# Softmax weights of forty steps transposed in 32x32 blocks by VectorE and regrouped through DRAM, in a fused attention and Fourier-mixing kernel

## The chip, the cores and the metric

The kernel runs on one core of a Trainium2 chip. The metric is the device time of one execution in microseconds (us). The median of three runs is 1605.03 us (1603.99 to 1605.74). One further execution was profiled; it took 1605.7 us, and its span, from the first to the last instruction of the profile, is 1603.8 us. All times of single instructions come from that execution.

## The reference

The inputs are q, k and v of shape (8 batches, 8 heads, 576 positions, 64), a scalar tau, w_ch1 (512 x 2048) and w_ch2 (2048 x 512), all in float32. In short:

```python
scores = matmul(q, k.transpose(0, 1, 3, 2)) / 8
scores = where(scores >= max(scores, -1) - tau, scores, -1e9)
attn = exp(scores - max(scores, -1))
x = matmul(attn / (sum(attn, -1) + 1e-9), v)      # heads side by side: (8, 576, 512)
u = x + real(fft(fft(x, axis=1), axis=2))
un = (u - mean(u, -1)) / sqrt(var(u, -1) + 1e-6)
out = u + maximum(un @ w_ch1, 0) @ w_ch2
```

## The kernel before

**Attention.** Two heads make a pair, and four pairs a batch, so there are 32 pairs. A pair is worked off in five steps (NT = 5): steps t = 0 to 3 hold 128 query positions of both heads, step 4 the last 64 positions of both heads side by side. A step n,t has the number i = 5n + t. For each step, `scores` multiplies q by k into PSUM (L427, L433 for step 4). `softmax_first` takes the row maxima on VectorE (L506) and the exponentials on ScalarE (L512, and L516 for the threshold). `softmax_second` applies the threshold and sums on VectorE (L527, L531, L534). `softmax_third` divides by the sum on ScalarE (L540). `weights_in_parts` then transposes the weights on TensorE, one block of 128x128 at a time: the tile `pe` (L578) holds the last 64 keys of both heads, and two tiles `pw` (L596) the 512 others of each head. That makes nine transposes a step, five for step 4. ScalarE copies them to SBUF (L584, L598, L600). `values_in_parts` multiplies them by v (L627): the first part, for positions 0 to 255, needs steps 0 and 1, the second part steps 2, 3 and 4.

**Mixing.** When the four pairs of a batch are done, their rows are folded by symmetry (`fold_rows`, L660), and `mixing` (L719) does both Fourier transforms with tables on TensorE and writes u, transposed, into the ring `u_t`.

**The two products with w1 and w2.** The 4608 rows of u are worked off in nine groups of 512. Group 0 uses plain products (`channels`). Groups 1 to 8 use `two_level`, a Strassen-Winograd scheme. For w1 it is one level: the product is split in four parts, and each part in seven blocks, m = 1 to 7, in the order of the list `ORDER`. Each block multiplies one combination of quarters of w1 by one combination of the tokens (b, t1, t2, t3, minus_t4), as four matmul calls at L1163, which the profile shows as eight instructions. `u_form` makes the combinations of tokens, on GpSimd except in the last two groups. Blocks 1, 6 and 7 share one bank of PSUM. Block 1 is copied out by ScalarE (L1172), as are blocks 5 (L1174) and 4 (L1182). Blocks 2, 6, 7 and 3 are added to the result by VectorE (L1100), and ScalarE applies the maximum with zero (L1105). The product with w2 has two levels, 49 blocks of four calls (L1306), with m in the order `L1` outside and `J` inside. There m = 1, 5 and 4 are copied by ScalarE (L1321), m = 2 is added by VectorE (L1323), and the others also by VectorE (L1326).

**Loads of the weights.** The combinations of w1 and w2 are made once (`w1_forms`, `w2_forms`), kept in DRAM as f1 and f2, and loaded again in each group into a ring of three buffers w1[0] to w1[2], of four blocks each (`PER = 4`, L1026; the loads are issued by `ensure`, L1030, at L1036). `block` asks for load n+2 when load n is first used.

**What sets the order of the work.** The order is written out by hand: every engine runs its instructions in the order of the program, and so does SP, from whose queue nearly all DMAs are issued. The pools decide only which buffer a tile gets. PSUM has four banks of tag `mm` for everything but scores, and four of tag `sc` for scores. From batch 3 on (counting from 1), the loop at L1635 runs one step of attention in each iteration and mixes in the other work: `fill` advances the products by a budget of work (`per_slot`) three times an iteration. Within an iteration i the order is: scores of i; the first or second part of the values, at t = 3 for the pair itself and at t = 1 for the pair before; maxima and exponentials; a first `fill`; weights and sums; the first half of the transposes of step i-1; a second `fill`; the second half; the division for step i; at t = 3 the transposes of q and k by VectorE (`prep_pair`, L398 to L401); a third `fill`. At t = 2 the transfers of v of the next pair are issued (`load_v`), and at t = 4 those of q and k of the pair after the next (`load_pair`), eight transfers together. After the second part of the values, `swap_rows` (L645) exchanges two rows of odd pairs by two DMAs out and two back, issued together.

After the last step of attention, at about 1370 us, the products of groups 7 and 8 run alone.

Of the kernel before, what the change touches and what calls it, by code (L numbers as in the profile page):

```python
# [47 lines left out]
def kernel(  # L48
# [48 lines left out]
    v_in = [const.tile([128, 10, D], FP32, name=f"v_in{u}") for u in range(2)]  # L97

# [24 lines left out]
    def load_pair(n, queue=nc.sync):  # L123
# [4 lines left out]
        raws = []  # L128
        for src, name, eng in ((q, "q_in", nc.sync), (k, "k_in", queue)):
# [10 lines left out]
            raws.append(raw)  # L140
        loaded[n] = raws
# [115 lines left out]
    w1 = [const.tile([128, HID], FP32, name=f"w1_{c}") for c in range(ND)]  # L257
# [181 lines left out]
    def softmax(i, between=None, meanwhile=None, behind=None):  # L439
# [43 lines left out]
        if normalized(i // NT):  # L483
            nc.vector.tensor_scalar(
                out=e[:, 0:S], in0=e[:, 0:S], scalar1=den[:, 0:1], scalar2=None, op0=ALU.mult
            )
            if nh == 2:
                nc.scalar.activation(
                    out=e[:, S : 2 * S], in_=e[:, S : 2 * S], func=ACT.Copy, scale=den[:, 1:2]
                )  # L490
        else:
            rec = sb.tile([128, 2 * D], FP32, tag="rec", name="rec")
            nc.gpsimd.tensor_copy(
                rec[:, :].rearrange("p (j d) -> p j d", j=nh), _repeated(den[:, 0:nh], 2 * D // nh)
            )
# [51 lines left out]

    def transposed_weights(i):
# [3 lines left out]
    def weights_in_parts(i):  # L552

        n, t = divmod(i, NT)
        e, rec = steps.pop(i)
        if t in (0, 2):
# [3 lines left out]
            e_t = sb.tile([128, 8, S - 256], FP32, tag="e_t", bufs=1, name="e_t")  # L560
            ends = sb.tile([128, 2, S - 256], FP32, tag="ends", bufs=1, name="ends")
            vt = heads[n][2]
            if t == 0 and PAIRS[n % NPAIR] % 2:

                vt = sb.tile([128, 10, D], FP32, tag="vr", bufs=1, name="v_rev")
                src = heads[n][2]
                nc.gpsimd.tensor_copy(vt[:, :, 0:1], src[:, :, 0:1])
                last = src[:, :, D - 1 : D]
                down = bass.AP(
                    tensor=last.tensor, offset=last.offset,  # L570
                    ap=[list(last.ap[0]), list(last.ap[1]), [-1, D - 1]],
                )
                nc.gpsimd.tensor_copy(vt[:, :, 1:D], down)
# [6 lines left out]
        if rec is not None:  # L580
            nc.tensor.transpose(pe[:, 1, :], rec[:, :], ident[:, :])
# [23 lines left out]
    def values_in_parts(n, part):  # L605
# [19 lines left out]
        for c in range(5):  # L625
            for j in range(2):
                nc.tensor.matmul(  # L627
                    pv[64 * j : 64 * j + 64, 0:m], vt[:, 2 * c + j, :],
                    e_t[:, 4 * j + c, 0:m] if c < 4 else ends[:, 0, 0:m],
# [3 lines left out]
        if normalized(n):  # L633
# [8 lines left out]
        if not (late and n % NPAIR == 0):  # L642
            swap_rows(n)

    def swap_rows(n):  # L645
        b, p = n // NPAIR, PAIRS[n % NPAIR]
        x = xs[b][p]
        if p % 2:
# [4 lines left out]
            for j in range(2):  # L653
                nc.sync.dma_start(out=x[64 * j : 64 * j + 1, :], in_=swap[1 - j : 2 - j, :])
# [217 lines left out]
    def channels(rows):  # L872
# [18 lines left out]
        def both():  # L891
            yield from w1_forms()
            ensure(1)
# [27 lines left out]
    ORDER = (1, 2, 5, 6, 4, 7, 3)  # L921
# [6 lines left out]
    def w1_forms():  # L928
# [6 lines left out]
        def keep(m, at):  # L935
            to = f1[:, :, :].rearrange("p (part m) (c n) -> p m c part n", m=7, c=2)
            for c in range(2):
                nc.sync.dma_start(
                    out=to[:, ORDER.index(m), c],
                    in_=quarters[at][c].rearrange("p (part n) -> p part n", n=256),  # L940
                )
# [23 lines left out]
        ensure(0)  # L965
# [60 lines left out]
    PER = 4  # L1026
    LOADS = [(f1, 28, k) for k in range(0, 28, PER)] + [(f2, 49, k) for k in range(0, 49, PER)]
    issued = 0

    def ensure(n):  # L1030

        nonlocal issued
        while issued <= n and issued < (NG - 1) * len(LOADS):
# [3 lines left out]
                out=w1[issued % 3][:, 0 : 512 * n_blocks].rearrange("p (j n) -> p j n", n=512),  # L1037
# [4 lines left out]
    def block(g, second, index):  # L1042

        n = len(LOADS) * (g - 1) + (7 if second else 0) + index // PER
        if index % PER == 0:
            ensure(n + 2 if g > 1 or second or index < 20 else n + 1)
        return w1[n % 3][:, 512 * (index % PER) : 512 * (index % PER + 1)]

# [13 lines left out]
    def two_level(g, rows):  # L1062
# [22 lines left out]
        def u_form(out_, in0, in1):  # L1085
            for c in range(2):
                (nc.vector if g >= NG - 2 else nc.gpsimd).tensor_tensor(
# [60 lines left out]
        for part in range(4):  # L1148
# [3 lines left out]
            sum_ = None  # L1152
            for at, m in enumerate(ORDER):
                left = block(g, False, 7 * part + at)
                if m in (6, 7):
                    bank = sum_
                else:
                    bank = ps.tile([128, 512], FP32, tag="mm", bufs=4, name="ph")
                if m == 1:
                    sum_ = bank  # L1160
                for q in range(2):
                    for c in range(2):
                        nc.tensor.matmul(  # L1163
                            bank[:, 256 * q : 256 * q + 256].rearrange(
                                "p (two n) -> p two n", two=2
                            ),
                            left[:, 256 * c + 128 * q : 256 * c + 128 * q + 128], right[m][:, c],
                            start=q == 0 and c == 0 and m not in (6, 7), stop=c == 1,
                            skip_group_check=True,
                        )  # L1170
                if m == 1:
# [572 lines left out]
```

## Time and profile before

| What | us |
|---|---|
| median of three runs | 1605.03 |
| the profiled execution: its time | 1605.7 |
| its span | 1603.8 |
| VectorE busy | 1105.6 |
| ScalarE busy | 908.4 |
| GpSimd busy | 811.7 |
| transposes of the weights (L596 and L578), as listed | 172.1 + 45.2 |
| row maxima (L506) and threshold (L527) from batch 3 on | 154.0 + 168.1 |
| DMA engines: mean share of the largest queue | 49.1% |

The page lists for each engine its busy time, then groups of instructions with their count, their sum, the mean of one in ns, the idle time of the engine just ahead of them, and what ended most of that idle time. A busy TensorE is not TensorE at its peak, since its instructions overlap: one starts before the one ahead of it has ended. Hence starts are compared with starts where the question is what an instruction takes from the engine. A window gives the busy time of each engine within a stretch of the span. The granted clock of TensorE was 0.988 over the span.

### The profile page before, as it was taken

Reading aid. Unit: us, or ns where it says so; the run is one execution under the profiler, and the core shown is the slowest. Engines: PE = TensorE matmul, PEld = TensorE weight load, DVE = VectorE, ACT = ScalarE, POOL = GpSimd, SP = SyncE. Lnnn points to the kernel's source line nnn. Section 1 sums busy time; section 2 is a strip of 40 time slices with the busy share of each in tenths; the row PEclk is TensorE's granted clock in tenths of the full one; section 3 lists DMA queues with packets and bytes.
Section 4 is the critical chain, followed back from the end, with each engine's and each line's share of the span. In section 5 each row is a group of like instructions: output and inputs, shape, how many; then the busy total and the mean of one; then the engine's idle time right before and its main releaser. Section 6 shows DMA issues by size and latency. Waiting matters only on the chain.

```text
span 1603.8 us, 27061 instructions
## 1 busy us (share of the span) xinstructions
PE 1537.4 (96%) x9770; PEld 1189.2 (74%) x9770; DVE 1105.6 (69%) x2165; ACT 908.4 (57%) x1873; POOL 811.7 (51%) x1014
## 2 busy tenths in 40 slices
PE   8999979999999999999999999999999999999997
PEld 4555445555787778877787878787887778879997
DVE  7997886845869566766577566856676656746547
ACT  5774665554655666656666666656665665223121
POOL 6784664034455552536254724455263625537646
PEclk9999999999999999999999999999999999999998
DMA  6423221555956264634564355626463534546655
GB/s 158 131 57 115 75 76 36 175 158 164 291 159 203 72 182 125 182 104 141 141 175 140 113 159 145 191 69 180 123 185 108 154 113 158 191 157 237 235 193 190
DMA packets 245499, 239.05 MB, mean 149 GB/s; under 512 B 196947, under 2 KB 214869, under 8 KB 225014
## 3 DMA queue, kind: packets, MB, share of 16 engines
q1 hardware_dynamic: 242854, 237.02, 49.1%
q8 instruction: 78, 1.28, 0.3%
q10 hardware_dynamic: 2512, 0.30, 0.2%
q14 instruction: 55, 0.45, 0.1%
HBM read 207.50 MB, written 29.62 MB: 148 GB/s over the span
## 4 chain that ended last, share of the span: by engine, by line
PE 76%; DVE 14%; ACT 4%; issue 2%; POOL 2%; DMA 1%; SPq 0%; DVEq 0%; ACTq 0%; POOLq 0%
PE ph L1163 24%; PE po L1306 17%; PE pv L627 8%; PE sc L427 7%; PE pw L596 6%; PE po L901 4%; PE ph L877 2%; PE py L750 2%; DVE e L467 2%; PE sc L433 1%; PE pa L767 1%; PE pe L578 1%; PE pa L771 1%; DVE neg L451 1%; ACT e L512 1%
## 5 line engine op out<-in xcount | busy, mean ns | idle before, releaser
L512 ACT ACTIVATE e<-sc,neg 128x576 f32<-128x576 f32 x216 | 158.6, 734 | 139.8 <-DVE neg L506 139.4
L506 DVE TENSOR_REDUCE neg<-sc 128x1 f32<-128x576 f32 x216 | 154.0, 749 | 112.0 <-PE sc L427 104.1
L1306 PE MATMUL po<-w,w_all 128*128 128x128 f32 x1792 | 229.1, 278 | 0.7 <-ACT ends L584 0.7
L1306 PEld LDWEIGHTS po<-w,w_all 128*128 128x128 f32 x1792 | 214.7, 193 | 10.2 <-issue 5.5
L1100 DVE TENSOR_TENSOR hs<-ph,hs 128x512 f32<-128x512 f32 (+1 forms) x128 | 105.1, 821 | 158.5 <-PE ph L1163 104.0
L1109 POOL TENSOR_TENSOR w<-hs 128x512 f32<-128x512 f32 x32 | 42.1, 1320 | 318.9 <-ACT hs L1105 245.1
L596 PE MATMUL pw<-ident,e 128*128 128x128 f32 x1152 | 172.1, 276 | 18.0 <-ACT x_first L634 9.1
L1163 PE MATMUL ph<-u_t,w 128*128 128x256 f32 x768 | 180.5, 381 | 0.5 <-DMA w<-f 0.4
L527 DVE SCALAR_TENSOR_TENSOR e<-sc,thr,e 128x576 f32<-128x576 f32 x216 | 168.1, 811 | 17.7 <-ACT thr L516 17.7
L427 PE MATMUL sc<-kT,qT 64*128 64x288 f32 x1024 | 170.3, 432 | 7.9 <-DVE e L467 7.9
L598 ACT COPY e_t<-pw 128x512 f32<-128x512 f32 x256 | 148.5, 594 | 45.8 <-PE pw L596 44.6
L540 ACT ACTIVATE e<-e,den 128x576 f32<-128x576 f32 x216 | 157.6, 775 | 16.6 <-DVE den L534 15.4
L596 PEld LDWEIGHTS pw<-ident,e 128*128 128x128 f32 x1152 | 136.3, 142 | 36.3 <-ACT x_first L634 10.1
L1163 PE MATMUL ph<-w_all,w 128*128 128x256 f32 x672 | 157.0, 382 | 2.9 <-DVE hs L1100 1.8
L1163 PEld LDWEIGHTS ph<-u_t,w 128*128 128x128 f32 x768 | 141.2, 190 | 23.4 <-issue 4.4
L1105 ACT ACTIVATE hs<-hs 128x512 f32<-128x512 f32 (+1 forms) x96 | 74.1, 772 | 122.0 <-DVE hs L1100 120.8
L1163 PEld LDWEIGHTS ph<-w_all,w 128*128 128x128 f32 x672 | 123.5, 190 | 25.6 <-issue 6.2
L427 PEld LDWEIGHTS sc<-kT,qT 64*128 64x128 f32 x1024 | 93.9, 186 | 62.9 <-issue 32.8
L1213 POOL TENSOR_TENSOR w_all<-w_all 128x128 f32<-128x128 f32 (+2 forms) x160 | 118.5, 758 | 29.9 <-DVE w_all L1326 22.4
L1306 PE MATMUL po<-w,hs 128*128 128x128 f32 x960 | 126.3, 279 | 0.0
L1306 PEld LDWEIGHTS po<-w,hs 128*128 128x128 f32 x960 | 116.2, 193 | 9.4 <-issue 7.2
L792 POOL TENSOR_TENSOR u_t<-x,tmp 128x289 f32<-128x289 f32 (+1 forms) x45 | 34.5, 766 | 104.8 <-DVE tmp L787 104.8
(221 smaller groups left out, 2985.1 us busy)
## 6 DMA issues: line engine op xcount, KB each, us to landing
w<-f SPq DMA_DIRECT2D x152, 1024.0 KB, 4.9
hs<-in_moe_w_ch_dram SPq DMA_DIRECT2D x23, 512.0 KB, 4.6
q_in<-in_q_dram SPq DMA_DIRECT2D x128, 72.0 KB, 3.9
out_dram<-u SPq DMA_DIRECT2D x36, 256.0 KB, 2.5
k_in<-in_k_dram SPq DMA_DIRECT2D x124, 72.0 KB, 3.0
v_in<-in_v_dram SPq DMA_DIRECT2D x64, 128.0 KB, 4.7
f<-w SPq DMA_DIRECT2D x14, 512.0 KB, 4.0
f<-w SPq DMA_DIRECT2D x7, 1024.0 KB, 4.4
```

Of the source, the lines that this page charges most:

```text
L427: nc.tensor.matmul(sc[j][:, c, 0:HALF], qT[hp, 128 * t : 128 * t + 128], kT[hp, k0 + HALF * c : k0 + HALF * (c + 1)], start=True, stop=True,)
L506: nc.vector.tensor_reduce(out=neg[:, j : j + 1], in_=sc[j][:, :, 0:HALF], axis=AXIS_XY, op=ALU.max, negate=True,)
L512: nc.scalar.activation(out=ej, in_=sc[j][:, :, 0:HALF], func=ACT.Exp, bias=neg[:, j : j + 1], scale=1.0)
L527: nc.vector.scalar_tensor_tensor(out=ej, in0=sc[j][:, :, 0:HALF], scalar=thr[:, j : j + 1], in1=ej, op0=ALU.is_ge, op1=ALU.mult, accum_out ...
L540: nc.scalar.activation(out=e[:, S * j : S * (j + 1)], in_=e[:, S * j : S * (j + 1)], func=ACT.Copy, scale=den[:, j : j + 1],)
L596: nc.tensor.transpose(pw[:, c, :], e[:, c0 : c0 + 128], ident[:, :])
L598: nc.scalar.copy(e_t[:, 4 * j : 4 * j + 4, qs], pw[:, :, :])
L627: nc.tensor.matmul(pv[64 * j : 64 * j + 64, 0:m], vt[:, 2 * c + j, :], e_t[:, 4 * j + c, 0:m] if c < 4 else ends[:, 0, 0:m], start=(c == 0 ...
L1100: nc.vector.tensor_tensor(out=to, in0=bank, in1=to if other is None else other, op=ALU.add)
L1163: nc.tensor.matmul(bank[:, 256 * q : 256 * q + 256].rearrange("p (two n) -> p two n", two=2), left[:, 256 * c + 128 * q : 256 * c + 128 * ...
L1213: return lambda: eng.tensor_tensor(out=to, in0=to, in1=other, op=ALU.add)
L1306: nc.tensor.matmul(to, lefts[m][j][:, s], right_[:, 128 * s : 128 * (s + 1)], start=(jn in (0, 4) or cut and jn > 4) and s == 0, stop=s == ...
```

## The change

The change has these parts.

- **Block transposes.** Of the steps of batches 4 to 8 with t = 0 to 3, those whose turn comes during the product with w1 (`phase[0] == 1`), 40 in all, are no longer transposed on TensorE. In the iteration after the step's own, and behind the softmax of that iteration, VectorE transposes its 128x1152 weights in blocks of 32x32 into `et_room`, a piece of w1[2] (`blocks`). SP writes that to one of three places in DRAM. In the iteration after that, SP fetches it back in four DMAs that put each block in the partitions where it belongs (`fetch`), into the tile `et_all`.
- **Layout of the weights.** From batch 4 on the transposed weights lie in `by_block`, a view of `et_all` with twelve blocks of 32 positions. Steps that TensorE still transposes are copied there by ScalarE; step 4 in more and smaller copies. The second part of the values is copied out in two pieces.
- **The first part of the values** of a pair moves from t = 3 to t = 4 where step 1 of the pair went by DRAM.
- **Order of the blocks with w1.** `FIRST` takes the place of `ORDER`: 1, then in each part 5, 2, 3, 4, 6, block 1 of the next part, 7. Block 2 is summed onto block 1 in PSUM, and block 3 onto block 5. ScalarE takes out the sum of 1 and 2 with the maximum, and then writes block 1 back into the bank from SBUF. VectorE adds only for blocks 6 and 7. t1 is made by VectorE.
- **Second product.** m = 2 is summed in PSUM onto the two banks of m = 1, which are kept, and copied by ScalarE.
- **Loads of w.** Five rooms of two blocks each (`PER = 2`), with load n+4 asked for when load n is first used.
- **Loads of q and k.** q of the next pair is requested at t = 0, and k at t = 1.
- **Swapped rows.** The two DMAs back are issued later in the iteration.

```diff
+    et_all = const.tile([128, 3 * SLOT], FP32, name="et_all")
+    by_block = et_all[:, :].rearrange("p (blk c q) -> p blk c q", c=NC9, q=32)
...
+    def decide(i):
+        n, t = divmod(i, NT)
+        by_dma[i] = i < B * NPAIR * NT and in_blocks(n) and t < 4 and (
+            phase[0] == 1 or t == 2 and by_dma[i - 1]
+        )
...
+    def blocks(i):
+        if not by_dma[i]:
+            return
+        e = steps.pop(i)[0]
+        out_ = et_room.rearrange("p (b c q) -> p c b q", b=4, c=NC9)
+        nc.vector.transpose(out_, e[:, 0 : 2 * S])
+        nc.sync.dma_start(out=scratch[i % 3][:, :], in_=et_room)
+
+    def fetch(i):
+        if not by_dma.get(i):
+            return
+        at = 9 * 32 * first_block(i % NT)
+        src = scratch[i % 3][:, :].rearrange("(a p) (b m) -> b p a m", p=32, b=4)
+        for b in range(4):
+            nc.sync.dma_start(
+                out=et_all[32 * b : 32 * b + 32, at : at + SLOT].rearrange(
+                    "p (a m) -> p a m", a=4
+                ),
+                in_=src[b],
+            )
...
-    ORDER = (1, 2, 5, 6, 4, 7, 3)
+    FIRST = [(0, 1)]
+    for part in range(4):
+        FIRST += [(part, m) for m in (5, 2, 3, 4, 6)]
+        FIRST += [(part + 1, 1)] if part < 3 else []
+        FIRST += [(part, 7)]
...
-    PER = 4
+    PER = 2
...
+    def ring(n):
+        room = n % 5
+        return w1[room // 2][:, 1024 * (room % 2) : 1024 * (room % 2) + 1024]
...
-            ensure(n + 2 if g > 1 or second or index < 20 else n + 1)
+            ensure(n + 4 if g > 1 or second else min(n + 4, 13 if index < 24 else 15))
...
-                (nc.vector if g >= NG - 2 else nc.gpsimd).tensor_tensor(
+                (nc.vector if g >= NG - 2 or out_ is t1 else nc.gpsimd).tensor_tensor(
...
+            base = {2: 1, 6: 1, 7: 1, 3: 5}.get(m)
...
+            if m in (1, 4):
+                nc.scalar.copy(h10, bank[:, :])
...
+            elif m == 5:
+                nc.scalar.copy(h11, bank[:, :])
+            elif m == 3:
+                nc.scalar.copy(h01, bank[:, :])
+            elif m == 2:
+                nc.scalar.activation(out=h00, in_=bank[:, :], func=ACT.Relu)
+                nc.scalar.copy(bank[:, :], h10)
+                background()
+            elif m == 6:
+                add(h01, bank[:, :])
+                relu(h01)
+            elif m == 7:
...
+                add(both, twice)
+                relu(both)
...
-        if t == 3 and i < total:
+        if t == (4 if by_dma.get(NT * n + 1) else 3) and i < total:
             values = values_in_parts(n, 0)
...
+        fetch(i - 2)
...
         if i < total:
             softmax_second(i)
         while held:
             held.pop(0)()
+        decide(i - 1)
+        blocks(i - 1)
+        while swaps:
+            swaps.pop(0)()
...
-        if t == 4 and n + 2 < B * NPAIR:
-            load_pair(n + 2)
+        if t < 2 and n + 1 < B * NPAIR and len(loaded.get(n + 1, ())) == t:
+            load_raw(n + 1, slice(t, t + 1))
```

## The prediction

> **What bounds the kernel now.** I read three views in this order: the page's busy times, the windows of one stage, and the timeline of TensorE in that stage.
>
> ```profile
> PE 1537.4 (96%) x9770; PEld 1189.2 (74%) x9770; DVE 1105.6 (69%) x2165; ACT 908.4 (57%) x1873; POOL 811.7 (51%) x1014
> L596 PE MATMUL pw<-ident,e 128*128 128x128 f32 x1152 | 172.1, 276 | 18.0 <-ACT x_first L634 9.1
> L1100 DVE TENSOR_TENSOR hs<-ph,hs 128x512 f32<-128x512 f32 (+1 forms) x128 | 105.1, 821 | 158.5 <-PE ph L1163 104.0
> ```
>
> TensorE is busy for 96% of the span, so what matters is what an edit takes from it or makes it wait for. The products with w1 (L1163) that run beside attention past the first batches stand at 551-631, 729-807, 900-980, 1074-1153 and 1249-1327 us. In the third:
>
> ```profile
> core 0: us, PE busy (x) PEld busy (x) DVE busy (x) ACT busy (x) POOL busy (x), PEclk, DMA share, GB/s
> 900.00:980.00 80.00, 80.00 (x455) 61.96 (x452) 49.90 (x101) 53.66 (x104) 33.67 (x57) 1.00 0.51 140
> ```
>
> TensorE never idles in these 80 us, VectorE has 30 us free, ScalarE 26 us, the DMA engines half. What an instruction really takes from TensorE is the distance from its start to the next start, as its listed duration overlaps the next one:
>
> ```profile
> 592.12 1.99 PE L1163 MATMUL ph<-u_t,w 128*128 128x256 f32 x8
> 593.95 0.27 PE L578 MATMUL pe<-ident,e 128*128 128x128 f32 x1
> 594.06 0.60 PE L596 MATMUL pw<-ident,e 128*128 128x128 f32 x4
> 594.50 1.89 PE L1163 MATMUL ph<-u_t,w 128*128 128x256 f32 x8
> 596.23 0.60 PE L596 MATMUL pw<-ident,e 128*128 128x128 f32 x4
> 596.66 1.89 PE L1163 MATMUL ph<-t_room,w 128*128 128x256 f32 x8
> ```
>
> Five transposes take 0.55 us, four 0.43, so the nine of a step take 0.98; a product block takes 1.73. By the same reading scores take 1.17, and the values 2.31 (first part) and 2.84 (second).
>
> **What the Trainium skill says.** "VectorE: DVE Perf Modes", section The three transpose paths: VectorE transposes only inside 32x32 blocks. The trace has this instruction on q and k (778 ns for 576 columns, 243 for 64), and never on the weights, so the regrouping needs another path. "DMA: Bandwidth & Descriptors", section Anatomy of one DMA: about 2.0 us of a DMA are fixed, mostly the receipt of the last byte, and waits are kept by the issuing sequencer, not by the DMA engines. The trace agrees in kind: 2.2 KB land in 1.7 us, 256 KB in 2.5. "TensorE: Matmul & The Clock Gate", Part 4: a transpose in a kernel takes about 275 ns; the row says 276, but the distance between starts is 0.11 us, and that decides here.
>
> **The change part by part.**
>
> *Transposes removed.* Instruction order of the changed kernel: 360 transposes fewer, eight steps in each of the five windows. 40 x 0.98 = 39.2 us gained, all on TensorE's path. An iteration there becomes scores and three blocks, 1.17 + 5.19 = 6.4 us.
>
> *Block transposes on VectorE.* From 576 and 64 columns: 1.05 ns a column, so 1152 columns take 1.38 us (bounds 1.2 and 2.0, the output being scattered in 32-element pieces). Eight in a window are 11 us; two of four product additions a part go (m=2, m=3: 8 x 0.69 = 5.5 less), and t1 comes (2 x 0.4). 49.9 + 11 - 5.5 + 0.8 = 56 us of some 75. On the path they cost nothing as long as TensorE has blocks to work on. Queued behind each are the next step's maxima (L506); where q and k are transposed as well (1.8 us) VectorE has 7.7 us of work in a 6.4 us iteration. The next, short step gives that back. With this cover gone it would cost up to 1.3 us in ten iterations, 13 us.
>
> *Copies.* ScalarE loses two copies of 0.59 and one of 0.26 a step (11.5 us a window), and takes two copies a part more (8 x 0.59) and finer ones for the fifth step (1.5). 53.7 becomes 48: nothing.
>
> *The round trip through DRAM.* This is the new wait. A step's blocks are written by VectorE in the next iteration, behind its softmax; SP writes them (590 KB), and in the iteration after that SP waits for the write and fetches four pieces of 147 KB. The first value product (now at t=4) needs the fetch of step t=1. Time to spare, for an undelayed TensorE: in an iteration, scores end at 1.2 us, maxima at 2.7, the second exponential at 3.7, weights and sums at 5.2, reciprocals at 5.7, blocks at 7.1. In the second pair of a window an addition of 1.23 us (m=7) stands ahead of the weights on VectorE, so it is 8.0. The value product is ready two iterations and 0.53 us of scores after the start of that iteration: 13.3, or 13.9 in the first pair with t1's wait. To spare: 6.8 us and 5.3 us. Needed: write 3.3 (2.5 for 256 KB, and 334 KB at the (4.4 - 2.5) us that 768 KB more cost); hand-overs 0.4; three issues ahead of the last at 0.5 each (v's rows), 1.5; landing of the last 2.8, between 2.3 (from the same line) and 3.3 (k in this window). Sum 8.0; bounds 7.0 and 10.5, the latter with the slow landings of this window:
>
> ```profile
> w<-f SPq DMA_DIRECT2D x8, 1024.0 KB, 5.4
> out_dram<-u SPq DMA_DIRECT2D x4, 256.0 KB, 2.4
> q_in<-in_q_dram SPq DMA_DIRECT2D x8, 72.0 KB, 5.4
> k_in<-in_k_dram SPq DMA_DIRECT2D x8, 72.0 KB, 3.3
> v_in<-in_v_dram SPq DMA_DIRECT2D x4, 128.0 KB, 4.9
> ```
>
> Waits: 1.2 + 2.7 = 3.9 us a window, 19.5 in five. Queued behind TensorE's wait is everything, as it runs in order. The second value product has some 11 us to spare: nothing.
>
> *New order of the blocks.* Part 3 ends with m=6 and m=7 side by side on one bank: m=7 waits for VectorE's addition from it. Matmul tail 0.16 + addition 0.69 + restart 0.1 = 0.95. Seven groups, and half of it in the first, where four transposes lie between: 7.2 us (bounds 5 and 14, if VectorE is in a softmax). The other new pairs (m=5 to m=3, m=1 to m=2, the bank refilled by ScalarE before m=6) have at least one block, 1.73, over a copy of 0.59: nothing. m=5 is now second and needs t1, hence t1 on VectorE behind two maxima: 0.5 a window, 2.5.
>
> *Second product.* m=2 is summed in PSUM: 16 additions less on VectorE, 16 copies more on ScalarE, two of four banks held for some ten blocks. Nothing; bounds 0 and 4 us for transposes that find no bank.
>
> *Queue of SP.* 152 loads of w more, of half the size, with the same lead of eight blocks (14 us of blocks, some 20 with attention) against 5.4 us of landing: nothing, also when SP is held for 5 us by a fetch or by the write's wait for VectorE. q and k are requested two iterations (13 us) ahead of use, not four; 2.4 us of issue and 5.4 of landing fit. The later write-back of swapped rows only moves 1.2 us of issue. Were SP held for 6 us more, k would be late.
>
> *Sum.* -39.2 + 19.5 + 7.2 + 2.5 = -10.0 us. The profiled execution took 1605.7 us (span 1603.8), 0.7 above the median of 1605.03; taken from the median, 1595.
>
> **Rivals.**
>
> *The round trip is hidden.* If VectorE's blocks come a microsecond earlier or DMAs land at their fastest (7.0 us), the waits fall to about 0.8 us a window: -39.2 + 4 + 9.7 = -25.5, 1579. For it: SP idles, and any other delay of TensorE in these iterations comes off the wait. Against: three loads are issued between write and fetch.
>
> *The round trip is late: slower.* Same place, the value product at t=4. Its price is 10 us a window for each microsecond in ten pairs; the gain is gone when the two waits of a window reach 5.9 us, a round trip of 9.0 instead of 8.0. For it: eight steps move 9.4 MB more a window, at 350 GB/s (the full slices of this window show 336 to 393) 27 us of DMA on top of 41, some 0.9 of 75 us, and landings of 5 us are seen at 0.51 already. At 9.7 us the waits are 7.3 a window: -39.2 + 36.5 + 9.7 = +7, 1612.
>
> *VectorE becomes the bound.* Its 56 of 75 us are against it; the tight iterations come just before the value product, so that their delay would lessen that wait and not add to it. At 13 us beside half the waits: -39.2 + 10 + 9.7 + 13 = -6.5, 1598.5. That the transposes stay is excluded by the instruction order.
>
> **How the numbers follow.** The forecast, a gain partly eaten by the round trip (1588 to 1601.8), VectorE's case among it: 0.40. Hidden, below 1588: 0.22. Late, above 1608.2: 0.23. Between, where waits and gain cancel: 0.15. A measurement here tells about 0.2%, 3.2 us, from no change. So faster 0.62, same 0.15, slower 0.23. The range, 1577 to 1613, leaves out the ends of hidden and late, a tenth each.
>
> **What would show it.** Right: windows of some 77 us instead of 80; first value products that start on a DMA, by 1 to 3 us, ten times; m=7 of part 3 waiting on VectorE for about 1 us; the block transpose near 1.4 us. Wrong: no DMA ahead of values (then 1579); landings of the pieces above 4 us (then 1612); TensorE waiting for scores' banks or copies instead, which I count at nothing; a block transpose of 2 us or more.

## The result, and the profile after

The changed kernel took 1686.43 us (median of four runs, 1680.35 to 1687.29) against 1605.26 of the kernel before: 1.0499 times as long, with a 95% interval of 1.0473 to 1.0525. It is 81 us slower, where 10 us faster was forecast. Its profiled execution took 1680.35 us, with a span of 1678.6. Line numbers are now those of the changed kernel: the blocks with w1 are L1288, VectorE's additions L1225, the values L730, and the transposes of the weights during the product with w1 L649 and L658.

The page, with busy times first and then one group of instructions:

```profile
PE 1522.1 (91%) x9410; PEld 1162.9 (69%) x9410; DVE 1128.3 (67%) x2137; ACT 905.5 (54%) x1913; POOL 814.2 (49%) x1002
...
L1225 DVE TENSOR_TENSOR hs<-ph,hs 128x512 f32<-128x512 f32 x64 | 60.6, 947 | 150.2 <-PE ph L1288 145.0
```

TensorE has 360 matmuls fewer, and its share falls from 96% to 91%: it waits. VectorE makes 64 additions in place of 128. The list of groups has the block transposes, and behind the bar the time that VectorE stood idle ahead of them and for what:

```profile
L601 DVE STREAM_TRANSPOSE w<-e 128x1152 f32<-128x1152 f32 x40 | 54.6, 1366 | 26.6 <-DMA e_blocks<-w 26.4
```

A block transpose takes 1.37 us, as forecast (1.38). But before 13 of the 40 VectorE stands idle until the write of the step before has landed, since there is only one room (`et_room`) for the blocks. The same stretch of work as before (the third window, here from 933 to 1027 us):

```profile
933.20:1026.60 93.40, 77.24 (x380) 56.86 (x379) 55.30 (x105) 48.91 (x97) 31.67 (x53) 0.91 0.72 202
```

It lasts 93.4 us, not 79.5 and not the 77 forecast. TensorE is busy for 77 of them, its granted clock is 0.91 instead of 1.00, and the DMA engines are at 0.72 instead of 0.51. What it waits for, over the whole span (total, times, longest):

```profile
PE pv L730 <- DMA et_all<-e_blocks: 75.7, 16, 9.4
```

There was no such wait before. Adding up TensorE's time in this window from start to next start, with the listed idle time kept apart, gives this account (us):

| third window | blocks | scores | values | transposes | idle | sum |
|---|---|---|---|---|---|---|
| before | 50.0 | 10.1 | 10.3 | 9.1 | 0.0 | 79.5 |
| after | 51.0 | 10.5 | 14.6 | 1.1 | 16.1 | 93.4 |

The transposes are gone as forecast (8.0 us a window). Against them stand 16.1 us of waiting and 4.3 us more for the same values. TensorE's timeline shows both at once:

```profile
945.85 1.13 PE L445 MATMUL sc<-kT,q_ends 128*128 128x288 f32 x4
955.58 4.53 PE L730 MATMUL pv<-et_all,v_rev 128*64 128x256 f32 x20 [8.59 <-DMA et_all<-e_blocks]
960.04 2.05 PE L1288 MATMUL ph<-u_t,w 128*128 128x256 f32 x8
```

After an idle time of 8.59 us the first part of the values takes 4.46 us to the next start, where it took 2.31. The windows of 4 us around it tell why (the column after POOL is the granted clock):

```profile
944.00:948.00 4.00, 2.98 (x14) 2.19 (x12) 0.43 (x4) 1.92 (x3) 3.92 (x8) 1.00 0.90 210
948.00:952.00 4.00, 0.00 (x0) 0.00 (x0) 2.10 (x3) 0.00 (x0) 3.92 (x10) 0.74 1.09 352
952.00:956.00 4.00, 0.42 (x2) 0.32 (x4) 2.98 (x6) 1.55 (x3) 1.30 (x3) 0.50 1.07 302
956.00:960.00 4.00, 4.00 (x20) 2.12 (x16) 1.74 (x5) 0.00 (x0) 0.00 (x0) 0.50 0.23 90
```

The clock is halved during the wait and stays so until the values are done. The Trainium skill says this ("TensorE: Matmul & The Clock Gate", HAM oscillation — how this bites in real kernels): where the wait for a DMA outlasts a window of about 3.4 us, the next stretch of matmuls starts at half clock. The trace agrees for the ten waits ahead of first parts, 4.35 to 9.43 us long, and the prediction left it out. The DMA engines, in the column beside the clock, are full during the wait. The landings in this window (how many, size of one, median time from issue to landing in us):

```profile
w<-f SPq DMA_DIRECT2D x14, 512.0 KB, 5.5
e_blocks<-w SPq DMA_DIRECT2D x7, 576.0 KB, 5.1
et_all<-e_blocks SPq DMA_DIRECT2D x28, 144.0 KB, 3.2
v_in<-in_v_dram SPq DMA_DIRECT2D x4, 128.0 KB, 5.1
swap<-x SPq DMA_DIRECT2D x4, 2.2 KB, 3.0
```

The write lands after 5.1 us at the median, where 3.3 was forecast. And in the first pair it starts late. VectorE finished the blocks of step 1 of this window's first pair at 939.42. SP's queue in that time:

```profile
937.25 1.17 SPq L759 DMA_DIRECT2D swap<-x  x2
940.63 1.13 SPq L763 DMA_DIRECT2D x<-swap  x2
941.82 2.19 SPq L140 DMA_DIRECT2D k_in<-in_k_dram  x4
944.05 0.50 SPq L1161 DMA_DIRECT2D w<-f  x1
944.59 0.43 SPq L602 DMA_DIRECT2D e_blocks<-w  x1
945.12 0.38 SPq L1161 DMA_DIRECT2D w<-f  x1
...
949.92 1.76 SPq L611 DMA_DIRECT2D et_all<-e_blocks  x4
```

SP is held by the exchange of two rows of the batch's first pair. `fold_rows` issues it, at once and not later: out (SP stood 5.5 us for GpSimd's copy of x, L779, before it could), wait for its landing (1.8 us), back. Behind it come k and a load of w, and only then, 5.2 us after the blocks were done, the write. From the end of the block transpose to the values it is 16.2 us (939.42 to 955.58). In the window's second pair SP writes at once (988.75, two hundredths after the blocks are done), and it is 11.2 us (988.73 to 999.91). The forecast was 8.0 for both.

### The profile page after: what moved, and what is told of

Read it like the earlier page. It is cut to its first block, busy times and chain, and to the rows that moved or that the text cites. A ratio compares the mean times of both kernels' runs of the same rounds, so it can differ in the third digit from the quotient of the medians.

```text
span 1678.6 us, 27057 instructions
## 1 busy us (share of the span) xinstructions
PE 1522.1 (91%) x9410; PEld 1162.9 (69%) x9410; DVE 1128.3 (67%) x2137; ACT 905.5 (54%) x1913; POOL 814.2 (49%) x1002
## 4 chain that ended last, share of the span: by engine, by line
PE 58%; DVE 17%; DMA 10%; ACT 6%; issue 4%; POOL 3%; SPq 2%; ACTq 0%; DVEq 0%; POOLq 0%
PE ph L1288 15%; PE po L1437 13%; PE pv L730 9%; PE sc L439 5%; DMA et_all<-e_blocks 4%; PE po L1015 3%; DMA w<-f 3%; DMA e_blocks<-w 2%; PE ph L991 2%; DVE e L539 2%; PE pw L641 2%; PE pw L694 2%; PE py L864 1%; DVE e L479 1%; ACT e L524 1%
## 5 line engine op out<-in xcount | busy, mean ns | idle before, releaser
L1288 PE MATMUL ph<-u_t,w 128*128 128x256 f32 x768 | 184.1, 384 | 0.0
L1288 PEld LDWEIGHTS ph<-u_t,w 128*128 128x128 f32 x768 | 141.7, 190 | 33.6 <-issue 12.3
L1288 PE MATMUL ph<-w_all,w 128*128 128x256 f32 x672 | 158.3, 383 | 6.0 <-DVE hs L1225 6.0
L1225 DVE TENSOR_TENSOR hs<-ph,hs 128x512 f32<-128x512 f32 x64 | 60.6, 947 | 150.2 <-PE ph L1288 145.0
L1288 PEld LDWEIGHTS ph<-w_all,w 128*128 128x128 f32 x672 | 125.1, 190 | 33.0 <-DVE hs L1225 8.8
L1230 ACT ACTIVATE hs<-hs 128x512 f32<-128x512 f32 x64 | 54.0, 843 | 158.3 <-DVE hs L1225 158.3
L730 PE MATMUL pv<-et_all,v_rev 128*64 128x256 f32 (+1 forms) x640 | 93.4, 443 | 44.2 <-DMA et_all<-e_blocks 41.6
L730 PE MATMUL pv<-et_all,v_in 128*64 128x256 f32 (+1 forms) x640 | 95.7, 449 | 36.2 <-DMA et_all<-e_blocks 34.1
L730 PEld LDWEIGHTS pv<-et_all,v_rev 128*64 128x64 f32 x640 | 48.4, 149 | 85.4 <-issue 39.0
L730 PEld LDWEIGHTS pv<-et_all,v_in 128*64 128x64 f32 x640 | 50.8, 151 | 78.2 <-issue 37.3
```

The source lines that it names most:

```text
L730: nc.tensor.matmul(pv[64 * j : 64 * j + 64, 0:m], vt[:, 2 * c + j, :], right, start=(c == 0), stop=(c == 4), skip_group_check=True,)
L1225: nc.vector.tensor_tensor(out=to, in0=bank, in1=to if other is None else other, op=ALU.add)
L1230: nc.scalar.activation(out=to, in_=to, func=ACT.Relu)
L1288: nc.tensor.matmul(bank[:, 256 * q : 256 * q + 256].rearrange("p (two n) -> p two n", two=2), left[:, 256 * c + 128 * q : 256 * c + 128 * ...
```

## The experiments

Three groups: what the rest of the change costs, what the round trip costs and why, and what could be saved. Times are medians; "before" was 1605.1 to 1606.7 in these comparisons.

### What the rest costs

**No step by DRAM (e1).** Everything else stays.

```diff
-        by_dma[i] = i < B * NPAIR * NT and in_blocks(n) and t < 4 and (
-            phase[0] == 1 or t == 2 and by_dma[i - 1]
-        )
+        by_dma[i] = False
```

> The changed kernel with no step sent through DRAM: TensorE transposes all weights, everything else of the change stays (new order of the w1 blocks, sums in PSUM, five rooms of two blocks, q and k in two steps). Theory (the round trip through DRAM is what is slow): the rest costs only the known small waits, m=7 on an addition (about 7 us) and t1 (2 us): 1605 to 1617 us, and no value product waits for a DMA. Rival (the rest of the change, with its longer chain of PSUM banks and its smaller loads of w, is what is slow): above 1650.

1626.45 us, 1.0128 times before (1.0113 to 1.0143). So the rest costs 21 us, twice the 9.7 forecast, and the 40 steps themselves make the kernel 60 us slower. A window lasts 81.9 us.

**Loads alone (e5):** the kernel before with the loads in pieces of two blocks, q and k in two steps, later write-back of swapped rows.

> The kernel before with one part of the change alone: loads of w in pieces of two blocks into five rooms, q and k of the next pair requested at t = 0 and t = 1, the swapped rows written back later. Block order, layout of the weights and transposes are those of before. My theory is that the 21 us which the change costs without its DRAM steps come from the new block order and the new layout, so that this kernel stays within 4 us of before (1601 to 1609 us). Rival: the loads are late (q and k are asked for two iterations ahead in place of four, and SP is held); then 1613 to 1622 us, with TensorE waiting for q, k or w.

1605.04 us, 0.9992 (0.9984 to 1.0001). The loads cost nothing.

**Order of the blocks and sums alone (e6):** the kernel before with `FIRST`, the sums in PSUM, and t1 on VectorE.

> The kernel before with another part alone: the new order of the blocks with w1 and their sums in PSUM, t1 on VectorE, and m = 2 of the second product summed in PSUM. My theory: m = 7 waits about 0.9 us for the addition of m = 6 in seven groups, t1 costs 0.3 us in five, and the halved clock after such waits some us more: 1611 to 1618 us. Rival: the order is harmless (under 1609 us), and the layout of the weights with its finer copies has the cost, which this kernel doesn't have.

1623.79 us, 1.0108 (1.0091 to 1.0125): above the forecast span, and 17 of the 21 us. TensorE's starts in the third window show five small stops, 2.4 us in all: t1 0.2; m = 7 of part 3 behind m = 6's addition 0.5; and three that I hadn't counted, at blocks that open a bank (m = 4 of part 0 0.35, m = 5 of part 2 1.0, m = 4 of part 2 0.3). The 1.0 ends with VectorE's addition of m = 7 of the part before, which is what frees a bank. So the two stops that were forecast (0.95 and 0.5) are there at half the size, and sums that hold a bank for longer, counted at nothing, cost more. Five windows at 2.4 us and 3.1 us in group 1 are 15 of the 17 us. What is left to e1, 2.7 us between the two medians, falls to the layout of the weights by elimination only: the five windows are as long in e1 as here (409.4 us together).

**The old order with all 40 steps (e13):** the changed kernel with the blocks, sums and t1 of before.

> The changed kernel with all its 40 steps by DRAM, but with the block order, the sums and t1 of the kernel before. If the cost of the new order simply adds, 1686 - 18 = 1663 to 1673 us. If TensorE's waits for the fetch cover it (a delay ahead of a wait comes off that wait), or VectorE needs the new order's relief, 1678 us or more.

1687.82 us, 1.0503 (1.0483 to 1.0524): no gain at all. The windows get shorter by 0.5 us on average (456.4 for five, against 458.7), where e6 had cost 2.4. So in the windows the new order is hidden: a delay ahead of a wait comes off that wait. The five stages with w2 (each from the end of a window to the next product with w1) get longer, 474.8 us against 459.6; why wasn't tested. Costs that were measured one at a time don't add here.

### What the round trip costs, and why

**Values that need no fetch (e2).** The first or second part multiplies v by a constant where a step of it went by DRAM, so those rows of the output come from the constant. All DMAs and block transposes stay.

```diff
-                if in_blocks(n):
+                if by_dma.get(NT * n + 2 * part) or by_dma.get(NT * n + 2 * part + 1):
+                    right = bass.AP(
+                        tensor=dim_s.tensor, offset=dim_s.offset,
+                        ap=[list(dim_s.ap[0]), [0, 2], [1, m // 2]],
+                    )
+                elif in_blocks(n):
```

> The changed kernel, in which the value products that need regrouped weights multiply a constant table in their place (those output rows are wrong for that reason). Block transposes, writes, fetches and their DMA traffic all stay; only TensorE's wait for the fetched weights is gone. Theory: the 360 transposes are now a net gain, 39 us less 7 and 2: 1570 to 1585, and the spells of half clock of TensorE go back to about those of before. Rival A (VectorE and DMA load of the path, not the wait, hold TensorE): above 1620. Rival B (the rest of the change): above 1650.

1634.1 us, 1.0182 (1.0156 to 1.0207). TensorE's wait for the fetch is worth 52 of the 81 us. But the time is some 50 us above the upper end of the forecast. About 12 of them are the rest of the change, which e1 showed to be dearer than thought. Some 25 are a wait of the blocks for VectorE, which is 32.9 us here and 8.4 in e1 (first TensorE's wait, then one of VectorE's; two views of this kernel):

```profile
PE ph L1293 <- DVE hs L1230: 32.9, 19, 4.7
```

```profile
DVE w L601 <- DMA e_blocks<-w: 48.6, 18, 5.8
```

Behind TensorE's first wait lies a second: VectorE waits for its room until the write has landed, the addition of m = 6 stands behind it, and m = 7 waits for that addition. In the changed kernel this fell into the wait for the fetch. What else makes up the 50 us stays open.

**v requested one iteration later (e4)**, behind the fetch (`t == 2` becomes `t == 3` ahead of `load_v`).

> The changed kernel with v of the next pair requested at t=3, behind the fetch, and no longer at t=2 between the write of step 1 and its fetch. Theory (in the second pair of a window the four issues of v, 3.5 us, and their transfers stand between write and fetch): both waits of a window get shorter by 1.5 to 3 us, 15 to 30 us in ten pairs, and the half clock after them less: 1645 to 1670. Rival (the write's own landing sets the fetch, SP's order does not matter): within 5 us of 1686.

1680.38 us, 1.0466 (1.043 to 1.0502): 6 us less, which the two intervals don't tell apart, and far less than forecast. The issues of v had mostly lain beside the landing of the write.

**Fewer exchanges (e12):** v one iteration later, and no exchange of rows from batch 3 on, except for the first pair of each batch. That exception was not meant: the exchange of the first pair is issued by `fold_rows`, which the edit didn't reach, and the expectation speaks as if all were gone.

> The changed kernel with less in SP's queue between a block transpose and its fetch: the exchange of two rows of odd pairs from batch 3 on is left out (these rows stay unexchanged), and v of the next pair is requested one iteration later. My theory: SP was held by the exchange in the first pair of a window, so its wait falls from 8.3 us to that of the second pair, 5.4, and both lose the 1.2 us that v's later request gave: the waits fall from 76 to 50 to 60 us, and the time is 1662 to 1672 us. Rival: only landings and VectorE count: within 5 us of the 1680 of v's later request alone.

1665.81 us, 1.0386 (1.0359 to 1.0414). The time was as forecast, but for another reason: the wait of the second pairs fell from 5.4 to 2.7 us, and that of the first pairs, which should have fallen, from 8.3 to 7.7 (6.7 to 9.4). Their exchange was still there, and the third window shows what it does with v out of the way:

```profile
928.61 1.13 SPq L763 DMA_DIRECT2D x<-swap  x2
929.79 2.19 SPq L140 DMA_DIRECT2D k_in<-in_k_dram  x4
932.03 0.50 SPq L1161 DMA_DIRECT2D w<-f  x1
932.57 0.43 SPq L602 DMA_DIRECT2D e_blocks<-w  x1
933.12 0.35 SPq L1161 DMA_DIRECT2D w<-f  x1
938.13 1.91 SPq L611 DMA_DIRECT2D et_all<-e_blocks  x4
```

The fetch follows the write after 5.56 us, so v's request isn't what makes that write land slowly.

**No exchange at all (e18).** Those rows stay unexchanged; v one iteration later.

```diff
-        if p % 2:
+        if p % 2 and not late:
...
-        if t == 2 and n + 1 < B * NPAIR:
+        if t == 3 and n + 1 < B * NPAIR:
             load_v(n + 1)
```

> The changed kernel without any exchange of two rows of odd pairs from batch 3 on (those rows stay unexchanged), v of the next pair requested one iteration later. In the run that left out only the exchanges issued inside the iterations, the second pair's waits fell from 5.3 to 2.7 us and the first pair's only from 8.3 to 7.7, with the first pair's exchange still ahead of its write. If that exchange is what holds SP, the write of the first pair goes out 4 to 5 us earlier, its waits fall to 2 to 4 us, and with them the halved clock after most of them: 1665.8 - 5 x 5 = 1641, less some 5 us of clock, 1632 to 1645 us. Rival: k's request, the loads of w and the landing take its place; first-pair waits of 6 us and more, 1655 us or more.

1622.62 us, 1.0094 (1.007 to 1.0118): 43 us less than with the first pairs' exchanges, and below the forecast span. Beside e12 the edit takes away the exchange of the first pairs and nothing else, and the whole gain lies in the five windows (396.8 us together, 440.4 in e12). All waits of values for a fetch are 28.2 us now, not 75.7; the first pairs wait 0 to 2.1 us, the second 2 to 3.2. SP's queue in the third window, at the same step:

```profile
907.25 2.05 SPq L140 DMA_DIRECT2D k_in<-in_k_dram  x4
909.39 1.20 SPq L1161 DMA_DIRECT2D w<-f  x1
915.01 0.34 SPq L602 DMA_DIRECT2D e_blocks<-w  x1
915.45 0.38 SPq L1161 DMA_DIRECT2D w<-f  x1
918.26 1.74 SPq L611 DMA_DIRECT2D et_all<-e_blocks  x4
```

k is long out when the blocks come, and the fetch follows the write after 3.25 us; in the changed kernel it was 5.33. The median landing of all writes fell from 4.8 to 3.4. The writes of step 1 in the first pairs, where the trace has their landing, took 5.5 to 6.0 us in e12, and 3.2, 3.2 and 4.9 here. So SP's hold cost twice: the write was late, and k, w, the write and w then went out one upon the other, within 4 us, and landed slowly. It cost a third time on VectorE, whose wait for its room is gone as well (26.4 us in the changed kernel, 25.9 in e12):

```profile
L601 DVE STREAM_TRANSPOSE w<-e 128x1152 f32<-128x1152 f32 x40 | 54.3, 1358 | 0.0
```

Step by step, v's request gave 6 us (e4), the exchanges of the second pairs 15 more (e12), those of the first pairs 43 (e18). A kernel that keeps the exchange, but issues it from another queue or behind the write, was not tried.

Even so e18 is slower than before. Its five windows are about as long as before (396.8 us, 398.0 before), as waits and the order of the blocks take back what the transposes gave. The loss is in the five stages with w2: 466.6 us, against 450.7 before and 453.3 without steps by DRAM (e1). TensorE idles there for 28.6 us instead of 18.3; the rest was not traced further.

**A quarter of the bytes (e11).** Write and fetches carry a quarter of the rows, so the values are computed from other data; number and order of DMAs stay.

```diff
-        nc.sync.dma_start(out=scratch[i % 3][:, :], in_=et_room)
+        nc.sync.dma_start(out=scratch[i % 3][0:32, :], in_=et_room[0:32, :])
...
                     "p (a m) -> p a m", a=4
-                ),
-                in_=src[b],
+                )[:, 0:1],
+                in_=src[b][:, 0:1],
```

> The changed kernel, whose DMAs carry a quarter of the rows: SP writes partitions 0 to 31 of the block transposes alone, and each of the four fetches brings a quarter of its pieces; the rest of the transposed weights is left as it was, so the values are computed from other data. The number of DMAs, their order and all waits stay. If the bytes, and the share of the DMA engines that they take, make the two landings long (5.3 and 4 us), these fall to 2.5 to 3 us each and TensorE's waits from 76 us to 25 to 45: 1632 to 1655 us. Rival: the queue of SP, what it waits for and what stands ahead, is what makes it late; then 1668 us or more.

1632.86 us, 1.0175 (1.0157 to 1.0193), with 33.0 us of waits and landings of 2.2 and 2.2 us instead of 4.8 and 3.4. The first pairs, where SP is still held, wait 4.4 to 5.7 us, the second 1.1 to 2.5. So the bytes are the other half: with short landings SP's hold costs less. The two gains, 54 us from bytes and 64 from SP's queue, are of the same waits and can't be added.

**Step 1 by TensorE (e3):** 30 steps by DRAM, t = 0, 2 and 3; the values back at t = 3.

> Step t=1 of each pair stays on TensorE, so that 30 steps and not 40 go through DRAM, and the first value product is back at t=3 and needs only the fetch of step 0, issued an iteration earlier. Theory: no value product waits for more than 1 us, and 30 x 0.98 = 29 us are gained less about 9: 1580 to 1595, faster than before. Rival (round trips of all steps are late, or the load of the path holds TensorE): above 1620.

1627.91 us, 1.0138 (1.0123 to 1.0153), far from the forecast 1580 to 1595. The wait moved: 14.3 us of values on DMAs, part of it in the second part, whose step 3 is fetched just as late, and m = 7 on VectorE 11.9.

**Values one iteration later (e7), and with two rooms (e8).** The first part is taken up at t = 0 of the next pair, with step 2's fetch behind it; e8 has a second room, and four rooms for w in place of five. First what was expected of e7:

> The changed kernel, in which the first part of the values of a pair that went by DRAM is taken up one iteration later (t = 0 of the next pair), and the fetch of its step 2, which goes to the same place, behind it. The round trip gains an iteration, 6.4 us or more. If my theory is right that the round trip is late by 4 to 9 us and that VectorE is held by its single room as well, the waits of the first value product fall from 76 us to under 15, m = 7 then waits for VectorE as it did when the values didn't wait at all (some 30 us), and the time is 1632 to 1650 us. Rival: the queue of SP is the bound, and everything moves back with it, so that waits of 4 us and more stay in each pair: 1660 us or more.

And of e8:

> As the kernel with the values one iteration later, and with two rooms for the blocks that VectorE transposes, so that it needn't wait for the write of the step before (the loads of w get four rooms of two blocks, with six blocks of lead, in place of five). If both waits, TensorE's for the fetch and VectorE's for its room, are what eats the gain, then 1626 less the 39 us of transposes, with up to 20 us of waits left: 1590 to 1610 us. Rival: transfers or VectorE are saturated, and a new wait takes the place of these: over 1622 us. If the shorter lead of w matters, TensorE waits for w.

1655.75 us, 1.0306 (1.0288 to 1.0325), and 1650.9 us, 1.0281 (1.0249 to 1.0314), both above what was forecast, and not told apart by their intervals. In e7 m = 7's wait for VectorE is 37.3 us, as forecast. In e8, 1590 to 1610 was forecast; m = 7's wait fell to 15.7, but TensorE now waits 44 us for DMAs. 27 of them lie ahead of the second part, whose step 2 is now fetched in the iteration before its use.

**Two rooms, values later, a quarter of the bytes (e14).**

> The kernel with two rooms and values one iteration later, whose DMAs carry a quarter of the rows (the values are computed from other data). If saturated transfers are why that kernel stays at 1651 us, its waits for DMAs (44 us) go and only m = 7's stay: 1595 to 1612 us. Rival: the wait has moved to the second part of the values by the order alone, whose fetch now starts in the iteration before its use: 1625 us or more.

1600.86 us, 0.9967 (0.9957 to 0.9978). With short landings the values' waits for these DMAs vanish, and the third window is 77.6 us; m = 7's wait of 15.7 stays. So with the fetches in time the change would pay, by 0.3%; but this kernel leaves out three quarters of the weights that it moves. Whether e8 without the exchanges comes near it wasn't tried.

### What could be saved

**Steps 0 and 2 alone (e9)**, 25 steps, each with an iteration to spare; the same in the old order of blocks **(e10)**; e10 in both products **(e15)**, 40 steps; e10 with the values copied ahead of the exponentials **(e16)**; and e16 with the second product's sums in PSUM **(e17)**. The edit of e9 is:

```diff
+        by_dma[i] = i < B * NPAIR * NT and in_blocks(n) and t in (0, 2) and (
+            phase[0] == 1 or t == 2 and by_dma[i - 2]
+        )
...
+        if t == (4 if by_dma.get(NT * n) else 3) and i < total:
```

Expected of e9:

> The changed kernel, but only steps 0 and 2 of each pair go by DRAM (about 20 in place of 40), and the first part of the values stays at t = 4, so that step 0 has a whole iteration more for its way and the first value product depends on no step that is just being fetched. VectorE's room and SP have two iterations for each write. My theory (the round trip is late for a step that is needed two iterations on, at 11 to 14 us): the waits for DRAM nearly vanish, below 10 us in all; from the 1626 us without DRAM steps some 20 us of transposes go: 1605 to 1616 us. Rival: any of these transfers makes others late (q, k, v, w) or holds VectorE and SP: 1625 us or more.

Of e10:

> As the kernel with steps 0 and 2 by DRAM, with the block order, the sums and t1 of the kernel before. These cost 17 to 18 us by themselves. If the costs add, the time is 1588 to 1600 us, faster than before. Rival: the new order is what gives VectorE the time for block transposes (it adds for two blocks in a part in place of four); then VectorE is late, TensorE waits for it, and the time is 1606 us or more.

Of e15:

> As the kernel with steps 0 and 2 by DRAM in the old order, but from batch 4 on in both products, 40 steps instead of 25. In the product with w1 these steps gave 2.7 us a window. If VectorE has time for them beside the second product too (it is busy for 72 of 96 us there), another 10 to 15 us: 1590 to 1600 us, faster than before. Rival: VectorE is what TensorE waits for there (scores' maxima, stores), and the time is 1606 to 1620 us.

Of e16:

> As the kernel with steps 0 and 2 by DRAM in the old order (25 steps), with one edit: ScalarE copies the values out before the exponentials, so that the bank is free when TensorE comes to the next block of the second product (it waited there for this copy four times, 5.0 us in all). Theory: 3 to 7 us less, 1600 to 1604.5 us. Rival: the exponentials are later for it and VectorE with them: 1607 us or more.

Of e17:

> Steps 0 and 2 by DRAM (25 steps), the old order with w1, ScalarE's copy of the values ahead of the exponentials, and m = 2 of the second product summed in PSUM. In the two kernels with steps 0 and 2 the five stages with w2 took 460.7 us with these sums (and the new order with w1) and 465.1 without. If the 4.4 us are due to the sums and add to the 1.3 us of the copies, 1607.6 - 5.7 = 1602 us, 0.2% below before; 1599 to 1604 us. Rival: the gain belonged to the pace of the new order, or two banks held for long make TensorE wait for a bank: 1606 us or more.

| | us | ratio to before (95%) |
|---|---|---|
| e9 | 1613.16 | 1.0046 (1.0031 to 1.0061) |
| e10 | 1607.61 | 1.0012 (1.0005 to 1.0019) |
| e15 | 1614.63 | 1.0053 (1.0038 to 1.0069) |
| e16 | 1606.26 | 1.001 (0.9998 to 1.0021) |
| e17 | 1607.67 | 1.001 (1.0003 to 1.0016) |

e9 is as forecast: no wait for a fetch is left, and the write lands in 3.2 us. The others miss. In e10 the window falls to 76.8 us, 2.7 below before, but the next stage gives it back: behind the third window the stage with w2 takes 97.0 us instead of 94.1, with 2.7 us more of idle TensorE, of which 1.3 waits for ScalarE's copy of the values. Copying first (1.3 us less) and the sums in PSUM (1.4 more again) change nothing beyond the intervals. In the stages it changes much: from e10 to e16 the five stages with w2 fall from 465.2 to 454.2 us, as hoped, but the five windows grow from 385.4 to 394.1, and TensorE now waits for ScalarE's division there, 1.5 us in most of them. The early copy in the stages with w2 alone wasn't tried. No version that computes everything beats the kernel before.

## Why the prediction was wrong

*Transposes removed* held: 8.0 us a window, 40 in five (39.2 forecast). *Block transposes*: their 1.38 us held (1.37). VectorE and ScalarE were busy in the third window for 55.3 and 48.9 us, where 56 and 48 were forecast. "On the path they cost nothing" held only in the shade of the larger wait; the room, which is bound to the write's landing, was overlooked (e2: 32.9 us of m = 7 waiting for VectorE, 8.4 in e1).

*The round trip through DRAM* and *Queue of SP* are the steps that failed. Waits of 19.5 us became 75.7, of which 68.5 stand ahead of the ten first parts that the forecast meant. The time to spare was right: 16.2 less 8.6 of waiting leaves 7.6 in the first pair (6.8 forecast), and 11.2 less 5.5 leaves 5.7 in the second (5.3). What was needed was wrong. In the third window SP's hold, the write, three issues and the last landing took 5.2 + 5.3 + 1.3 + 4.3 = 16.1 us in the first pair and 0 + 5.5 + 1.3 + 4.4 = 11.2 in the second, not 8.0. "Hand-overs 0.4" assumed that SP is idle when the blocks come. In the first pair it is held for another 5.2 us, by an exchange that the trace of the kernel before shows too, in the first microseconds of the same window:

```profile
903.99 1.17 SPq L652 DMA_DIRECT2D swap<-x  x2
906.39 1.13 SPq L654 DMA_DIRECT2D x<-swap  x2
```

There nothing urgent stood behind it. I had reckoned SP's hold against k and w, but not against the write that the change itself puts into the same queue. The landing of the write, 3.3 forecast, was 5.3 in the first pair and 5.5 in the second (988.75 to the fetch at 994.21), and that of the last piece some 4.4 instead of 2.8. With SP free (e18) the write took 3.4 us at the median, the first pairs waited 0 to 2.1 us and the second 2 to 3.2, near the 1.2 and 2.7 forecast. The Trainium skill, "DMA: Bandwidth & Descriptors" (Anatomy of one DMA), has a fit of 2.0 us and the bytes at 436 GB/s, made for DMAs that GpSimd issues; SP issues these. As an estimate it gives 3.35 us for this write: near what was measured with 25 steps (3.2) and with SP free (3.4), too little for the changed kernel (4.8). The fit's fixed part is more than the smallest DMAs took here: 2.2 KB landed in 1.7 us.

The rival "late" had the right mechanism, and its price holds, a microsecond of waiting for each microsecond of round trip (10 us for all ten pairs; "a window" is a slip): in the third window the two round trips were 8.2 and 3.2 us longer than forecast, and the two waits grew by 10.2, from 3.9 to 14.1. But it put the round trip at 9.7 us, and no bound went beyond 10.5. The load of the DMA engines came as it said: 41 + 27 = 68 us of a window were forecast, and 0.72 of 93.4 us is 67. So it was when the requests went out, and not their sum, that was missed. *Not priced at all* was the halved clock after a long wait: the values took 69.1 us in the five windows, in place of 51.5.

*New order and t1*, 9.7 us forecast, cost some 17 alone (e6), through banks that came free late, and nothing measurable where TensorE waits anyway (e13). *Loads of w, q and k* at nothing: right in the kernel before (e5). *Second product* at nothing: not measured by itself; its sums gained nothing in e17.

Not settled: how the 64 us that e18 gains over the changed kernel divide between late starts, slow landings and the clock.

## What to carry to other kernels

When a change puts a transfer with a due time into a queue, list what that queue does in the same microseconds, the small old DMAs that wait on an engine above all: they cost nothing until something urgent stands behind them. Price a wait of TensorE with the halved clock that can follow it. And follow the buffer: a single room ties the engine that fills it to the landing of the last write. In e2 this reached TensorE, once its own larger wait was gone; in e18, with the queue free, VectorE didn't wait for its room at all.

## What the runs showed that was not expected

- The same write of 576 KB landed in 3.2 us (e9), 3.4 (e18) and 4.8 (changed kernel), at mean DMA shares in the third window of 0.65, 0.88 and 0.72; a quarter of it in 2.2. The kernel with the largest share is not the one with the slowest landing, so the mean share doesn't tell how long a write takes.
- After each of the ten waits of 4.35 to 9.43 us the clock stayed halved into the work that followed: a first part of the values, listed with 2.38 us at full clock, took 3.8 to 4.5 where the trace has all of it. Shorter waits can do it too. In e18 waits of 2.1, 2.2 and 2.6 us were followed by 3.6 to 4.1 us, with a granted clock of 0.50, but others of 2.1 to 2.4 and of 3.2 us were not.
